# A chunked recurrence ahead of a mixture of experts: the start-up and the order within a unit are changed

## The chip, the cores and the metric

The kernel runs on one core of a Trainium2 chip. The metric is the device time of one execution in microseconds; the change is judged by the median of several runs beside runs of the kernel before. A profile of one execution shows the core's engines: PE (TensorE, matmuls), DVE (VectorE), ACT (ScalarE), POOL (GpSimd) and SP (SyncE, which here only issues transfers).

## What is computed

A linear recurrence with a decaying state per head, and then a mixture of eight experts with two chosen per token:

```python
def _attn_ref(r, k, v, w, a, b):            # 4 batches, 8 heads, 768 steps, 40 wide
    for t in range(S):
        y[:, :, t] = np.einsum('bhd,bhde->bhe', rt, state)
        Sa = np.einsum('bhde,bhe->bhd', state, at)
        state_decay = state * wt[:, :, None, :] - np.einsum('bhd,bhe->bhde', Sa, bt)
        state = state_decay + np.einsum('bhd,bhe->bhde', vt, kt)

def _moe_ref(x, w_gate, w_noise, noise, w1, w2):   # 3072 tokens, 320 wide, hidden 1024
    noisy_logits = x @ w_gate + np.log1p(np.exp(x @ w_noise)) * noise
    # the two largest of 8, softmax over the two, then for each expert e
    h = np.maximum(x[mask] @ w1[e], 0.0)
    out[mask] += top2_w[mask, k, None] * (h @ w2[e])
```

## The kernel before, in words

The 768 steps are cut into 12 chunks of 64, and the 32 sequences into two halves of 16. A chunk of one half is a unit; there are 24 units (NU), which go through one after the other, the halves in turn. Within a unit the recurrence is matrix work on 64 x 64 blocks.

For each unit u, ahead of time (up to LP = 8 units): w, a and kb (k and b) are loaded into rings; `ln` (ACT) takes the logarithm of w into one of two tiles L and uc; `sm` (PE) sums it along the chunk by a triangular matrix; `ex` (ACT) takes exp of the sum with either sign, and POOL copies one column of it to gam; `lc` (DVE, tile lm) takes the largest logarithm, for a check at the end. `aprod` and `kprod` (x = 1 and x = 0) multiply a and kb by these in place, on POOL in the loop and on DVE at the start. `LS` (PE) forms a triangular 64 x 64 matrix, its closure evicts it on ACT into la, `LSd` copies a quarter of it.

The inverses of these matrices are made for four units at a time: `xtr` (DVE transposes), `solve` (DVE, 30 elimination steps of two instructions, dealt out over the units by the tables PLAN and PLAN1 to three places A, B and C of a unit), `tout` (two DVE transposes back, and a POOL memset). `TA` and `TB` (PE) join 32-blocks to 64. The first four units take smaller blocks (`solve16`, 14 steps, `tout16`) and join them in `S16a` and `S16b` on PE with evictions on ACT between and after.

Unit n of the loop in `run` issues on PE, in this order: Y(n-1), W2(n), TA(n) with two fillers, LS(n+7), TB(n), AK(n+1), U(n), KBT(n+1), sm(n+8), UT(n), RL(n-1), W1(n+1), P(n), ST(n+1) with two fillers; up to n = 2 also S16(n+1) after P. A filler (`warm`) is a 128 x 512 matmul on zeros whose output nobody reads. Evictions follow on ACT: w of W2, two of TA (dr), tt of TB, ln(n+8), la of LS, uc and two pm of U, two utm of UT, kt of KBT, LSd, xr of RL, two exps of ex(n+8), z of S16a, two pm of vc, St of ST. On DVE stand the state's sum S and xT after Y, lc, akm after AK, the logit reduce lg after RL, pm after P, and the solve steps: C after Y, B before RL, A at the end of the unit. POOL scales the state by gam right after S, and does aprod and kprod and, from unit 9 on, the scatters of the routing.

The order on each engine is the order of the calls (`manual_schedule`); each engine and each queue works in that order, and `after` adds a wait on an instruction. `s.ea` is the last ACT instruction, on which loads of the loop are made to wait. PSUM has three tiles of the kind p2 and two of the kind p1.

Ahead of the loop `ramp` does constants, loads and the first four units, and ends in `first`, which is unit 0 with the products of units 4 to 8 in between. Behind unit 23 the experts follow; the tables for them are loaded in units 15 to 21.

## Time and profile before

| | us |
|---|---|
| median of 3 runs | 818.46 (816.27 to 822.21) |
| the profiled execution | 817.96 |
| its span, first to last instruction | 816.0 |
| start and units 0 to 3 (to the filler of unit 4's TA) | 116.5 |
| units 4 to 15 | 174.1 |
| units 16 to 23 and the joint with the experts (to 402) | 111.3 |
| the experts | 414.0 |
| busy over the span: PE, DVE, ACT, POOL | 728.5, 516.5, 391.0, 337.8 |

A matmul in float32 is recorded as several instructions, so sm's four are eight. In the views `rw` holds the ring of w, `ra` that of a, `rk` that of kb, and `X__71` the tile of the elimination. [...] The chain of waits goes back from the last instruction to what released each one.

### The profile page before, as it was taken

The numbers are of one execution on the slowest core, as the hardware profiler recorded it, in microseconds if no ns is written. First come the engines' busy times: TensorE is split into PE (matmuls) and PEld (weight loads), VectorE is DVE, ScalarE is ACT, GpSimd is POOL, SyncE is SP. The second block draws the span as 40 slices with busy tenths as digits, with TensorE's granted clock in tenths as the row PEclk, the third lists the DMA queues.
The fourth block names the chain that finished last, engine by engine and source line by source line (L and its number), as shares of the span: only waits on it lengthen the run. The fifth ranks groups of instructions, "written<-read, shape, count | busy, mean of one in ns | idle before, by whom it ended". The sixth has DMA issues, their size and how long they took to land.

```text
span 816.0 us, 29101 instructions
## 1 busy us (share of the span) xinstructions
PE 728.5 (89%) x12619; PEld 537.9 (66%) x12619; DVE 516.5 (63%) x1083; ACT 391.0 (48%) x837; POOL 337.8 (41%) x463
## 2 busy tenths in 40 slices
...
GB/s 203 57 163 112 106 135 140 159 137 156 119 143 143 168 125 58 107 125 82 92 74 100 163 71 184 111 122 114 134 94 144 20 124 117 41 13 26 28 18 40
DMA packets 67700, 87.06 MB, mean 107 GB/s; under 512 B 15641, under 2 KB 52461, under 8 KB 67565
## 3 DMA queue, kind: packets, MB, share of 16 engines
...
HBM read 63.41 MB, written 21.69 MB: 104 GB/s over the span
## 4 chain that ended last, share of the span: by engine, by line
PE 67%; DVE 14%; ACT 10%; issue 5%; DMA 2%; another core or an unknown queue 0%; SPq 0%; POOL 0%; ACTq 0%; DVEq 0%; POOLq 0%
PE po L369 21%; PE ph L354 21%; PE py L782 3%; PE sm L589 2%; PE pt L334 2%; DVE Tt L635 2%; DVE X__71 L636 2%; PE kt L710 2%; DVE pm L768 2%; PE tb L696 2%; PE pp L766 2%; ACT la L524 2%; PE ta L686 1%; PE rl L795 1%; DVE dr L639 1%
## 5 line engine op out<-in xcount | busy, mean ns | idle before, releaser
L377 POOL DMA_INDIRECT out_dram<-y,le x45 | 74.6, 1658 | 189.7 <-ACT y L371 186.6
L354 PE MATMUL ph<-rw__68,rk 128*128 128x384 f16 (+1 forms) x512 | 97.0, 339 | 3.7 <-DVE hl L356 1.8
L354 PE MATMUL ph<-dr,la 128*128 128x448 f16 (+1 forms) x384 | 85.8, 339 | 1.4 <-issue 1.4
L369 PEld LDWEIGHTS <-rk 128*128 128x128 f16 x576 | 56.5, 99 | 36.9 <-issue 7.3
L182 POOL DMA_INDIRECT ls<-ent,po x48 | 50.2, 1045 | 70.3 <-ACT pm L524 44.5
L354 PEld LDWEIGHTS <-rk 128*128 128x128 f16 x512 | 49.5, 98 | 40.5 <-issue 4.5
L371 ACT ACTIVATE y<-po,le 128x320 f32<-128x320 f32 (+1 forms) x53 | 26.6, 504 | 93.0 <-PE po L369 74.5
L356 DVE SCALAR_TENSOR_TENSOR hl<-ph,hh 128x448 f16<-128x448 f32 x64 | 39.2, 621 | 44.8 <-ACT hh L355 44.3
L355 ACT ACTIVATE hh<-ph 128x448 f16<-128x448 f32 x64 | 34.0, 543 | 64.8 <-PE ph L354 63.6
L636 DVE TENSOR_TENSOR X__71<-X__71,Tt 128x30 f32<-128x30 f32 (+9 forms) x150 | 60.8, 405 | 5.5
L635 DVE TENSOR_TENSOR Tt<-X__71 128x30 f32<-128x30 f32 (+9 forms) x150 | 60.8, 406 | 3.7
L355 ACT ACTIVATE rk<-ph 128x384 f16<-128x384 f32 x64 | 30.7, 488 | 62.5 <-PE ph L354 43.8
L242 DVE TENSOR_REDUCE yc<-y 128x1 f32<-128x320 f32 (+1 forms) x53 | 23.8, 456 | 57.3 <-ACT y L371 56.8
L369 PEld LDWEIGHTS <-hh 128*128 128x128 f16 (+1 forms) x640 | 46.5, 103 | 18.5 <-issue 2.0
L356 DVE SCALAR_TENSOR_TENSOR rk<-ph,rk 128x384 f16<-128x384 f32 x64 | 34.4, 552 | 34.0 <-ACT rk L355 22.5
L354 PEld LDWEIGHTS <-la 128*128 128x128 f16 x384 | 37.2, 98 | 27.3 <-issue 1.6
L782 PE MATMUL py<-pm,kt 128*64 128x104 f32 (+1 forms) x768 | 42.8, 262 | 7.3 <-DVE pm L768 3.8
L594 POOL COPY gam<-B 104x8 f32<-104x8 f32 x24 | 5.3, 220 | 105.7 <-ACT B L524 104.9
L369 PE MATMUL po<-ra,rk 128*128 128x320 f16 x288 | 46.0, 306 | 3.0 <-ACT rk L355 2.5
L782 PEld LDWEIGHTS py<-pm,kt 128*64 128x64 f32 x768 | 36.8, 142 | 10.9 <-DVE pm L768 5.0
L607 POOL TENSOR_TENSOR rk<-rk,B 104x512 f32<-104x512 f32 x31 | 36.9, 1189 | 13.2 <-DVE X__71 L636 9.0
L369 PE MATMUL po<-w2h,rk 128*128 128x320 f16 x192 | 33.7, 302 | 3.7 <-issue 2.6
...
## 6 DMA issues: line engine op xcount, KB each, us to landing
...
```

Source lines behind the costliest of these rows:

```text
L182: st=nc.gpsimd.indirect_dma_start(out=s.ls,out_offset=OFFS(ap=po[:,j,k:k+1],axis=0),in_=s.ent[:,j,k],in_offset=None)
L242: s.nc.vector.tensor_reduce(s.yc[q:128,s.ny:s.ny+1],a,axis=AX.X,op=ALU.add); s.ny+=1
L354: for i,(a,b) in enumerate(mm): s.hmm=nc.tensor.matmul(ph[:,:n],a,b,start=i==0,stop=i==7)
L355: s.hrelu=nc.scalar.activation(hh[:,f],ph[:,:n],AF.Relu)
L356: s.hhl=nc.vector.scalar_tensor_tensor(hl[:,f],ph[:,:n],0.0,hh[:,f],op0=ALU.max,op1=ALU.subtract)
L369: for j in range(c): nc.tensor.matmul(po[p*j:p*j+p,:d],h[:,f,r],w[:,f,d*j:d*j+d],start=k==0,stop=k==23)
L371: s.hy=nc.scalar.activation(y[:,:d],po[:,:d],AF.Copy,scale=w_[:,ii:ii+1])
L377: st=s.nc.gpsimd.indirect_dma_start(out=o[0],out_offset=OFFS(ap=o[1],axis=0),in_=o[2],in_offset=None,compute_op=ALU.add)
L607: s.after((eng or s.nc.gpsimd).tensor_tensor(z,z,b1,op=ALU.mult),e)
L635: eng.tensor_tensor(t,X[:,j:j+1,j+1:].to_broadcast([128,j,m]),X[:,0:j,j:j+1].to_broadcast([128,j,m]),op=ALU.mult)
L636: s.hs=eng.tensor_tensor(X[:,0:j,j+1:],X[:,0:j,j+1:],t,op=ALU.add)
L782: nc.tensor.matmul(pp[64*y:64*y+64,b,128*hh:128*hh+n],kt[:,j,y],m[:,y,j,0:n],start=first and hh==0,stop=True,skip_group_check=True)
```

## The change

**At the start.** Two w tiles are loaded first and each later w one unit earlier than before. Constants are cleared in another order, some by POOL rather than DVE or ACT; the clearing of vt, r and rb goes from ACT (`null`) to POOL. Five fillers on a cleared tile wz stand ahead of the first sm, two after most of the following steps (WU), and 24 (WR) between W1(0) and sm(6), while DVE eliminates. The loop over the first four units is written out as a pipeline: sm of the next unit goes ahead of the products of this one; the gamma copies of units 0 to 5 go to DVE.

**lc.** For units from 4 on the DVE reduce becomes a Square on ACT with the sum as a second output, ahead of the two exps in `ex`; units 0 to 3 keep the reduce (`lcv`).

**Joining.** S16 is taken apart: S16a stands behind KBT's eviction, S16b behind P.

**The unit.** ln, sm and ex of unit n+9 go to the end of unit n, behind ST; LSd follows LS's eviction at once. kprod x=1 of unit n+8 stands first in the unit and waits for the last A step of the unit before (hA), the scaling of the state (`Sg`) and aprod wait for the last C step, or for xT where there is none (hC), kprod x=0 waits for the logit reduce (hl). ST's fillers are kept only where no unit lies eight ahead, and unit 16 gets the four fillers FL too. In `first` P(0) comes ahead of the products of unit 7; unit 1 does sm, ex and kprod of unit 9 as well.

```diff
-FT,FS,FL,FU=2,2,4,2
+FT,FS,FL,FU,WR,W0,WU=2,2,4,2,24,5,2
-        s.z=t([128,160],F32,name="z"); V.memset(s.z,0.0)
-        s.d1=t([128,8,65],F16,name="d1"); s.mk32=t([128,1,32],F32,name="mk32")
+        s.d1=t([128,8,64],F16,name="d1"); s.wz=s.fl(s.d1)[:,0:128]; V.memset(s.wz,0.0); s.z=t([128,160],F32,name="z")
+        s.mk32=t([128,1,32],F32,name="mk32")
         s.L=[t([128,4,2,64],F32,name="L"),s.uc]; s.TR=t([128,136],F32,name="TR")
-        V.memset(s.a[0],0.0); V.memset(s.kb[0],0.0); V.memset(s.L[0],0.0); V.memset(s.a[1],0.0); V.memset(s.kb[1],0.0); V.memset(s.L[1],0.0)
+        V.memset(s.L[0],0.0); V.memset(s.a[0],0.0); V.memset(s.kb[0],0.0); V.memset(s.L[1],0.0)
         G.memset(s.TR,0.0)
-        G.memset(s.a[2],0.0); G.memset(s.kb[2],0.0); G.memset(s.gt,1.0); G.memset(s.lm,0.0); G.memset(s.a[3],0.0); G.memset(s.kb[3],0.0)
+        V.memset(s.z,0.0)
+        G.memset(s.a[1],0.0); G.memset(s.kb[1],0.0); G.memset(s.lm,0.0); G.memset(s.gt,1.0); G.memset(s.a[2],0.0); G.memset(s.kb[2],0.0); G.memset(s.a[3],0.0); G.memset(s.kb[3],0.0)
...
+        if i==2:
             for z in s.kt: G.memset(z,0.0)
-            G.memset(s.mk32,1.0)
-            for q in range(4): G.affine_select(out=s.mk32[32*q:32*q+32,0],in_=s.mk32[32*q:32*q+32,0],pattern=[[-1,32]],base=0,channel_multiplier=1,compare_op=ALU.is_gt,fill=0.0)
-            G.memset(s.d1,0.0)
-        if i==1:
-            for q in range(4): G.tensor_copy(s.i32[32*q:32*q+32],s.m.idm[32*q:32*q+32,32*q:32*q+32])
+            G.memset(s.fl(s.d1)[:,128:512],0.0)
             for z in s.w: G.memset(z,0.0)
-            G.memset(s.dg,0.0)
-        if i==2:
-            G.memset(s.rp,0.0); G.memset(s.iw,0.0)
+            G.memset(s.iw,0.0)
+    def warm0(s,pp,k):
+        for _ in range(k): s.nc.tensor.matmul(pp,s.wz,s.wz[:,0:1].to_broadcast([128,512]),start=True,stop=True)
...
     def lc(s,u):
-        s.nc.vector.tensor_reduce(s.lm[:,u:u+1],s.L[u%2 if u<7 else 0][...,0:40].rearrange("p h y e->p (h y) e"),axis=AX.XY,op=ALU.max,apply_absolute_value=True)
-    def sm(s,u):
-        pp=s.Sp=s.p1t("sm"); L=s.L[u%2 if u<7 else 0]
+        s.act(s.fl(s.wq[u%NW])[:,0:320].rearrange("p (h y e)->p h y e",h=4,y=2),s.L[u%2 if u<7 else 0][...,0:40],AF.Square,accum_out=s.lm[:,u:u+1])
+    def sm(s,u,t=None):
+        pp=s.Sp=s.p1t("sm") if t is None else t[:,0]; L=s.L[u%2 if u<7 else 0]
+    def lcv(s,u):
+        s.nc.vector.tensor_reduce(s.lm[:,u:u+1],s.L[u%2][...,0:40].rearrange("p h y e->p (h y) e"),axis=AX.XY,op=ALU.max,apply_absolute_value=True)
     def ex(s,u):
+        if u>3: s.lc(u)
         z=s.Sp.rearrange("p (j t)->p j t",t=64); B=s.B[u%2][:,0:520].rearrange("p (j c)->p j c",c=65)
         s.act(s.wq[u%NW][:,:,0:64],z,AF.Exp,scale=-1.0)
         s.act(B[:,:,0:64],z,AF.Exp)
-        s.nc.gpsimd.tensor_copy(s.gam[0:RF,u],B[0:RF,:,0])
+        if u>5: s.nc.gpsimd.tensor_copy(s.gam[0:RF,u],B[0:RF,:,0])
-    def aprod(s,u,eng=None,h=None):
-        R=slice(0,RF); h=slice(0,8) if h is None else slice(4*h,4*h+4); a=s.a[u%NAB][R,h]
-        (eng or s.nc.gpsimd).tensor_tensor(a,a,s.wq[u%NW][R,h,0:64],op=ALU.mult)
+    def aprod(s,u,eng=None,e=None):
+        R=slice(0,RF); a=s.a[u%NAB][R]
+        s.after((eng or s.nc.gpsimd).tensor_tensor(a,a,s.wq[u%NW][R,:,0:64],op=ALU.mult),e)
...
-        if u and u+LP<NU: s.sm(u+LP)
         pp=s.p1t("ut")
-        if not u or u+LP>=NU: s.warm(pp,FU)
+        if u+LP>=NU: s.warm(pp,FU)
...
-        pp=s.p1t("st"); s.warm(pp,FS); S=s.S[u%2]
+        pp=s.p1t("st"); s.warm(pp,FS if u+LP>=NU else 0); S=s.S[u%2]
...
-                nc.gpsimd.tensor_tensor(Sv,Sv,gb,op=ALU.mult)
-        nc.vector.tensor_tensor(x.rearrange("p (h b) t->p b h t",b=2),pv[...,0:64],s.wq[u%NW][:,:,0:64].rearrange("p (h b) t->p b h t",b=2),op=ALU.mult)
+                s.sg=(Sv,gb)
+        s.hx=nc.vector.tensor_tensor(x.rearrange("p (h b) t->p b h t",b=2),pv[...,0:64],s.wq[u%NW][:,:,0:64].rearrange("p (h b) t->p b h t",b=2),op=ALU.mult)
+    def Sg(s):
+        if s.sg is not None: s.after(s.nc.gpsimd.tensor_tensor(s.sg[0],s.sg[0],s.sg[1],op=ALU.mult),s.hC); s.sg=None
...
-            for u in us: load(u); s.lw(u+1)
+            for u in us: load(u); s.lw(u+2)
             s.ea=e
-        s.lw(0); loads(0,1,2,3); LS={}
-        s.ln(0); s.sm(0); s.ex(0); s.ln(1); s.sm(1); gn(4); s.consts1(0)
-        for u in range(4):
-            if u<3: s.ex(u+1)
-            s.aprod(u,V); s.kprod(u,1,None,V); s.kprod(u,0,None,V); s.lc(u)
-            if u==3: s.lc(4); V.tensor_reduce(s.m16,s.i32[:,16:32],axis=AX.X,op=ALU.add)
-            if u>1: s.lmask(u-2)
-            if u==0: loads(4); gn(5,6)
-            if u==1: s.consts1(1); gn(7,8)
-            if u==2: s.consts1(2); G.memset(s.a[9],0.0)
-            if u<3: s.ln(u+2); s.sm(u+2)
-            LS[u]=s.LS(u)
-            if u: LS[u-1](); s.LSd(u-1)
-        LS[3](); s.LSd(3); s.lmask(2); s.AK(0); s.lmask(3); s.ex(4); s.ln(5); s.sm(5); s.ex(5); s.xtr(0)
-        s.consts1(3); s.xmask16()
-        s.ea=None; s.lv(0); loads(5,6)
+        s.lw(0); s.lw(1); loads(0,1,2,3); LS={}
+        s.warm0(s.p1t("wm"),W0)
+        def vp(u): s.aprod(u,V); s.kprod(u,1,None,V); s.kprod(u,0,None,V); gc(u)
+        def gc(u): V.tensor_copy(s.gam[0:RF,u],s.B[u%2][0:RF,0:520].rearrange('p (j c)->p j c',c=65)[:,:,0])
+        f=s.p2("wm")[:,0]
+        s.ln(0); s.sm(0); s.Sq={0:s.Sp}; s.lcv(0); s.ln(1); s.warm0(f,WU); s.sm(1); s.Sq[1]=s.Sp; s.lcv(1); s.consts1(0)
+        def ex(u): s.Sp=s.Sq[u]; s.ex(u)
+        ex(0); vp(0); s.ln(2); s.warm0(f,WU); s.sm(2); s.Sq[2]=s.Sp; gn(4); ex(1); s.lcv(2); loads(4)
+        LS[0]=s.LS(0); vp(1); s.ln(3); s.sm(3); s.Sq[3]=s.Sp; LS[0](); s.LSd(0); s.consts1(1); G.memset(s.dg,0.0); s.warm0(f,WU)
+        ex(2); s.lcv(3); LS[1]=s.LS(1); vp(2); s.lmask(0); ex(3); LS[1](); s.LSd(1); gn(5); G.memset(s.rp,0.0); s.warm0(f,WU)
+        LS[2]=s.LS(2); V.tensor_reduce(s.m16,s.i32[:,16:32],axis=AX.X,op=ALU.add); vp(3); s.lmask(1); s.ln(4); LS[2](); s.LSd(2); s.warm0(f,WU); LS[3]=s.LS(3); s.AK(0); s.sm(4); s.lmask(2)
+        LS[3](); s.LSd(3); s.lmask(3); s.ex(4); s.ln(5); s.sm(5); gc(4); s.ex(5); s.xtr(0); gc(5)
+        s.consts1(2); gn(6); s.consts1(3); s.xmask16()
+        s.ea=None; s.lv(0); loads(5)
+        for z in s.vt+s.r[:1]+s.rb[:1]: G.memset(z,0.0)
+        gn(7,8)
+        for z in s.r[1:]+s.rb[1:]: G.memset(z,0.0)
+        G.memset(s.a[9],0.0)
         m.consts2(s.z)
-        s.KBT(0)(); s.consts16(); s.ln(6)
-        s.W1(0)
-        for z in s.vt+s.r+s.rb: s.null(z)
-        s.ea=None; H('gv',s.vt,0); H('gr',s.r,0); H('grb',s.rb,0); s.lv(1); load(7); s.lw(8); load(8)
+        s.KBT(0)(); s.consts16(); s.ln(6); s.W1(0)
+        s.warm(s.p1t("wm"),WR)
+        s.sm(6,s.p2("sm"))
+        s.ea=None; H('gv',s.vt,0); H('gr',s.r,0); H('grb',s.rb,0); s.lv(1); loads(6); load(7); load(8)
...
-        s.lw(LP+1); load(LP+1); H('gr',s.r,1); H('grb',s.rb,1); s.lv(2)
+        s.lw(LP+1); load(LP+1); H('gr',s.r,1); H('grb',s.rb,1); s.lv(2); s.lw(LP+2)
...
-        s.vprods(4); s.vprods(5); s.lc(5); s.lc(6)
-        s.S16a(0); s.S16b(0); s.sm(6); a4=s.LS(4); s.W2(0); s.ex(6); s.TA(0); a4(); s.ln(7); a5=s.LS(5); s.TB(0); s.vprods(6)
-        s.sm(7); a5(); s.U(0); s.LSd(4); k=s.KBT(1); s.UT(0); s.ex(7); s.lc(7); s.vprods(7)
-        a6=s.LS(6); s.LSd(5); k(); s.ln(LP); s.lc(LP)
-        s.P(0); s.S16a(1); a6(); s.LSd(6); s.AK(1); s.Y(0); a7=s.LS(7); s.S16b(1); s.sm(LP); a7(); s.LSd(7); s.ex(LP)
+        s.vprods(4); s.vprods(5)
+        s.S16a(0); s.S16b(0); a4=s.LS(4); s.W2(0); s.ex(6); s.TA(0); a4(); s.ln(7); a5=s.LS(5); s.TB(0); s.vprods(6)
+        s.sm(7); a5(); s.U(0); s.LSd(4); k=s.KBT(1); s.UT(0); s.ex(7)
+        a6=s.LS(6); s.LSd(5); k(); s.ln(LP)
+        s.P(0); s.vprods(7); s.S16a(1); a6(); s.LSd(6); s.AK(1); s.Y(0); a7=s.LS(7); s.S16b(1); s.sm(LP); a7(); s.LSd(7); s.ex(LP)
         s.ld(H,1,'gv',s.vt)
-        s.xtr(1); s.xmask(); s.aprod(LP,V); s.kprod(LP,1,None,V)
-        s.W1(1); s.vc(1); s.hA=None
+        s.xtr(1); s.xmask(); s.aprod(LP,V); s.kprod(LP,1,None,V); s.kprod(LP,0,None,V)
+        s.ln(LP+1); s.W1(1); s.vc(1); s.lnx=LP+1; s.hA=None
...
-            if n and ok(n+LP-1): s.kprod(n+LP-1,0,s.hA)
+            if ok(n+LP) and n>1: s.kprod(n+LP,1,s.hA)
+            s.hs=s.hx
             if n>1: s.Y(n-1); sv('C')
+            s.hC=s.hs
+            if n>1: s.Sg()
             if n and not q and n<=20: m.rstep()
             if ok(n): s.W2(n); s.TA(n)
-            s.ld(s.lw,n+LP+1)
+            if n==1: s.sm(LP+1); s.ex(LP+1); s.kprod(LP+1,1)
+            s.ld(s.lw,n+LP+2)
             ls=s.LS(n+LP-1) if n>1 and ok(n+LP-1) else None
-            if n>1 and not ls: s.warm(s.p2('wm')[:,0],FL)
+            if not ok(n+LP): s.warm(s.p2('wm')[:,0],FL)
...
             if ok(n): s.TB(n)
-            if n and ok(n+LP): s.ln(n+LP); s.lc(n+LP)
-            if ls: ls()
-            if ls and not q: s.LSd(n+LP-1)
+            if ls: ls(); s.LSd(n+LP-1)
+            if n==1: s.LS(LP)(); s.LSd(LP)
...
-            if n and ok(n+1): s.AK(n+1)
+            if ok(n+1): s.AK(n+1)
+            if ok(n+LP): s.aprod(n+LP,None,s.hC)
...
-            if n==1: ls=s.LS(LP); ls()
             if kb: kb()
-            if ls and q: s.LSd(n+LP-1)
+            if n<3: s.S16a(n+1)
...
-            if n==NU-1: s.turn(0); s.act(s.gt[:,8*NU:9*NU],s.lm,AF.Exp)
+            if n==NU-1: s.turn(0); s.act(s.gt[:,8*NU:8*NU+4],s.lm[:,0:4],AF.Exp); s.act(s.gt[:,8*NU+4:9*NU],s.lm[:,4:NU],AF.Exp,scale=0.03)
...
             if ok(n-1): s.RL(n-1)
             cut()
             sc(1)
-            if n and ok(n+LP): s.ex(n+LP); s.kprod(n+LP,1)
             if ok(n+1): s.W1(n+1)
+            if ok(n+LP): s.kprod(n+LP,0,s.hl)
             if ok(n): s.P(n)
-            if ok(n+LP): s.aprod(n+LP)
-            if n<3: s.S16(n+1)
+            if n<3: s.ln(n+1+LP); s.S16b(n+1)
...
             sv('A'); s.hA=s.hs
             if solving and q==3: s.tout()
             s.ld(s.lv,n+2)
+            if ok(n+1+LP) and n>=3: s.ln(n+1+LP)
             if ok(n+1): s.ST(n+1)
+            if ok(n+1+LP): s.sm(n+1+LP); s.ex(n+1+LP)
```

## Rows read from the trace of the kernel before

**Rows 1.** Windows: busy time (instructions) of PE, PEld, DVE, ACT, POOL, clock, DMA.
```profile
66.94:85.08 18.14, 16.17 (x521) 13.61 (x517) 15.09 (x31) 11.06 (x27) 7.08 (x8) 0.88 0.34 104
...
103.21:116.53 13.32, 12.70 (x394) 10.99 (x388) 10.71 (x25) 8.66 (x20) 3.51 (x5) 1.00 0.38 111
116.53:290.67 174.14, 155.97 (x4676) 134.63 (x4671) 146.63 (x334) 105.51 (x248) 83.24 (x117) 0.99 0.51 147
...
402.00:816.00 414.00, 384.94 (x2813) 247.72 (x2804) 219.12 (x402) 156.07 (x295) 162.65 (x144) 0.98 0.40 87
```

**Rows 2.** Windows over two stretches at a low granted clock, the columns as before.
```profile
34.00:47.00 13.00, 6.54 (x202) 5.62 (x202) 12.08 (x23) 9.61 (x21) 4.14 (x26) 0.50 0.38 121
...
64.00:68.00 4.00, 4.00 (x55) 2.77 (x52) 1.67 (x1) 3.76 (x10) 0.19 (x1) 0.57 0.23 62
```

**Rows 3.** Timeline of the start: begin, us, engine, line, operation, out<-in, count, idle before.
```profile
0.80 1.28 ACT L528 ACT_TABLE_LOAD   x1 [0.80 <-PEq L1083]
...
3.90 2.04 PE L589 MATMUL sm<-TR,L 128*128 128x128 f32 x8 [3.90 <-POOL lm L539]
...
22.40 0.60 ACT L524 ACTIVATE la<-ls 128x512 f32<-128x512 f32 x1 [1.90 <-PE ls L614]
23.02 0.84 ACT L524 ACTIVATE la<-la 32x256 f32<-32x256 f32 x2
...
28.26 0.15 DVE L657 TENSOR_TENSOR Tt<-X__71 128x28 f32<-128x28 f32 x1
...
38.14 1.14 ACT L544 ACTIVATE r<-z 128x512 f32<-128x512 f32 x2
...
40.26 1.11 DVE L664 MEMSET dr<- 32x512 f32 x2 [0.16 <-DMA vt<-in_gv_dram]
...
47.36 0.69 PE L686 MATMUL ta<-dr,la 32*32 32x32 f32 x32
...
55.22 0.69 DVE L601 TENSOR_TENSOR ra<-ra,rw__68 104x512 f32<-104x512 f32 x1 [4.66 <-ACT rw__68 L524]
55.83 1.29 DVE L607 TENSOR_TENSOR rk<-rk,B 104x512 f32<-104x512 f32 x2
...
58.19 1.22 DVE L768 TENSOR_TENSOR pm<-pp,mk 128x1024 f32<-128x1024 f32 x1
```

**Rows 4.** Chain of waits at the start: begin, us, what.
```profile
3.44 4.07 DMA rw__68<-in_gw_dram
```

**Rows 5.** Chain of waits in unit 1, around S16.
```profile
77.53 0.49 ACT B L524
...
80.38 0.54 PE st L568 x2
```

**Rows 6.** Chain of waits in unit 6.
```profile
149.73 0.89 PE sm L589 x8
...
153.72 0.54 PE st L568 x2
...
155.32 1.58 PE py L782 x32
```

**Rows 7.** Chain of waits in unit 10.
```profile
201.22 0.61 DVE xT L792
...
203.34 0.48 ACT L L524
...
203.84 0.48 DVE lm L586
...
205.01 0.59 DVE akm L707
```

**Rows 8.** Timeline of unit 6, then a group by form (count, sum, mean ns).
```profile
154.77 1.18 POOL L607 TENSOR_TENSOR rk<-rk,B 104x512 f32<-104x512 f32 x1
...
154.94 1.25 DVE L635 TENSOR_TENSOR Tt<-X__71 128x220 f32<-128x220 f32 x1
...
L635 DVE TENSOR_TENSOR Tt<-X__71 128x240 f32<-128x240 f32 x10 | 4.0, 404 | 0.2
```

6 lines of the change are left out of this document (5 added, 1 removed).

## The prediction, made before the result was known

> **What bounds the kernel now.** I read the windows first. Attention fills the span to about 402 us; the experts take the other 414 us and no line of theirs is edited [rows 1]. So the change can only move the left part, and the experts' start moves with it. Inside attention there are two unlike stretches. Up to 116.5 us, four units are solved at start-up and units 0 to 3 go through; units 1 and 2 last 18.1 us each, unit 3 13.3 us. Units 4 to 15 take 174.1 us, 14.5 us each, with PE busy 156 and DVE 147 of them [rows 1].
>
> At the start no engine is full. PE is slow: eight sm matmuls take 2.04 us there and 0.89 us in unit 6 [rows 3, 6]. [...] The chain from 0 to 41 us then alternates between ACT, PE's sm and, from 28.3 to 41.4, DVE's elimination with its transposes [rows 3].
>
> In units 4 to 8 the chain runs along PE, one unit after another, with hardly a gap; a filler of 0.54 us before ST stands in it [rows 6]. In units 9 to 15 it runs along DVE. Unit 10 shows why: after xT, DVE waits through TB, its eviction and ACT's ln for the lm reduce, and akm starts 3.2 us after xT ended [rows 7].
>
> **A. To the start of the elimination (28.26 us now).** w of units 0 and 1 are issued together, so ln(1) no longer waits for a load that was issued at 3.44 and landed 4.07 us later [rows 4]; now ln(2) is the first that waits for such a load, to about 7.6. POOL clears a1 and kb1 now and each load still stands behind its own memset, so SP's order costs nothing that the w2 load doesn't show. From there ACT's list is what is left: ln of units 2 to 5 (4 x 0.48), pairs of exp for units 1 to 5 (5 x about 1.0), the evictions of LS with their copies (4 x (0.60+0.84)), two Squares and the last sm's wait (about 1.5) [rows 3, 5, 7]. That is 14.2 us, to 21.8; the gamma copy and the mask on DVE add 0.6. The elimination would start near 22.4, not 28.26: 5.8 us. This needs the fast PE. If the fillers don't raise the clock, six sm (12.4) and fifteen fillers of about 0.5 (1.0 for a pair at the low level, twice the 0.54 of [rows 6]) stand on PE from 3.9 on, and the gain is 0 to 2. I take **4.0**, nearer to the list, as loads may be late.
>
> **B. Elimination to TA(0) (28.26 to 47.36).** DVE's part, to 41.37, is untouched [rows 3]. After it PE now does S16b, sm(6), LS(4) and fillers, all at the low clock, for 6.0 us. The 24 new fillers and sm(6) run under DVE's 13.1 us and cost nothing there; without that cover they would cost 24 x 0.27 = 6.5 us. The five clearings (0.57 each, of which [rows 3] has two) go from ACT to POOL: they held back S16a's eviction, and SP's loads of v, r and rb stand behind POOL's memsets now. POOL is through with them by about 30 by my addition, earlier than the 38 to 40 on ACT. What is left after DVE: the products of unit 4 (0.69+0.64, first of the two kprods [rows 3]), LS(4) of about 0.7, the filler pair 0.54: 2.0 to 2.6 us rather than 6.0. I take **3.0**; 2.5 if the clock is low then.
>
> **C. TA(0) to unit 3.** In `first`, pm(0) stands on DVE behind the products of unit 7, which wait for their exp till 55.22, and starts at 58.19 [rows 3]; P comes before them in the new order: up to 2.7 us. The joining: in unit 1 the chain has 2.4 us between the end of the exp and ST, S16's two halves with an eviction between them [rows 5]; unit 2 shows 2.3. With S16a before RL and S16b after P, RL, W1 and P lie over that eviction. [...] Against this unit 1 gets sm and ex of unit 9 as well (0.9 on PE, some 1.5 on ACT). With the stalls gone the units should come near unit 3's present 13.3 [rows 1]: 18.14+18.13-13.5-13.3 = 9.5, and 2 in `first`: 11.5. Bounds: 5, if the low stretches stay, and 15. I take **9.5**.
>
> **D. Units 3 to 15, and the later ones.** Removed from PE: a filler pair of 0.54 per unit up to 14. sm moves behind ST, into the time in which PE waits for pm in any case: pm takes 1.2 [rows 3], and fillers, ST and Y's first half now fill 1.6 between P and Y's second half [rows 6]. But sm needs ln(n+9), which is behind vc on ACT. ACT works 8.8 us a unit (105.5 over 12 [rows 1]); by my estimate three quarters of it stand in one unbroken list from tt to that ln, and L is ready some 0.5 us after ST has ended, so PE waits there: of the 0.54 I count 0.3 in units 4 to 8, 1.5 us. Removed from DVE: the lm reduce of 0.48 and its wait. In unit 10 akm could start when AK is through, some 1.5 us sooner [rows 7]; where PE binds instead, nothing. Added to ACT: a Square with a sum. No row shows one; the bounds are 0.48 (the ln of the same size [rows 7]) and twice that, if the sum is a piece of its own, and I take 0.5, hidden, as ACT is busy 106 of 174 us [rows 1].
>
> POOL's products now wait for DVE: kprod x=1 for the last step of the elimination, the state's scaling and aprod for the C steps, kprod x=0 for the logit reduce. Behind them on POOL stand the scatters; LS a unit later and ST wait for the products, with over 3 us to spare. On SP the w load of unit n+10 takes the ring's place of unit n-1 and so waits for xT at the start of unit n; the loads of a, kb, r and v behind it are needed a unit or more later, so I count nothing. What POOL's waits may give: a DVE step of 220 elements took 1.25 us beside a POOL kprod of 1.18, where one of 240 takes 0.40 on average [rows 8]; each such meeting costs DVE some 0.85, and three products a unit can meet it. Beside S, xT and pm, which read PSUM, it is not seen (pm 1.22 [rows 3]). [...]
>
> Units 9 to 15: 1.0 us each, 7. Minus 1.0 for a set of four fillers new in unit 16, minus 0.5 for odds and ends: **7.0**. Bounds: -3 (fewer fillers, two more falls of the clock at 1.7 us, nothing else gained) and +15. Units 17 to 23 keep all their fillers and I count nothing.
>
> **The sum.** 4.0+3.0+9.5+7.0 = 23.5 us off the span of 816.0 gives 792.5. The median shown, 818.46, is 2.5 above that span (the profiled execution itself is given as 817.96): **795.0**. The parts' bounds are unlikely to fall together; the likeliest case's own range is 783 to 804.
>
> **Rivals.** *The unit's new order gives nothing.* sm at the end waits for ACT, fewer fillers let the clock fall more often. [...] Against: DVE's chain in units 9 to 15. Then D is -3: 805.
>
> *The start stays slow.* The fillers don't bring the clock up, or let it fall before DVE is through. For: from 34 to 47 us PE worked half the time and stayed at the low level. Against: from 64 to 68 it was busy throughout and the clock came back inside that stretch [rows 2]. Then A is 0, B 2.5, C 6: 803. With both, 813.
>
> *Slower: the Square needs another table.* The trace has one table load, 1.28 us at the start [rows 3], for Ln, Exp and Copy. If Square is not in that set, two loads stand before each pair of exp from unit 4 on, 2.6 us on ACT in some 20 units. ACT's 8.8 us a unit plus 0.5 plus 2.6 still fits 13, but ex comes right before W2's eviction: 0.8 to 2.6 us a unit, 16 to 51 in all, so 811 to 846, say 830. It decides once two loads exceed the 2 us or so that ACT has free there. [...]
>
> **How the numbers follow.** The likeliest case 0.57, the order gives nothing 0.16, the start stays slow 0.11, both 0.09, the table 0.05, something else 0.02. A measurement here can tell about 1%, so faster is below 810.3 and slower above 826.6. The first three cases are faster; so is a third of "both"; the rest of it and a little of the table case are within 1%. Faster 0.87, same 0.08, slower 0.05. The range goes from the likeliest case's low end over both single rivals: 783 to 809.
>
> **What would show it.** A: the elimination's first step near 24 us, sm near 0.9 to 1.1 us from the second or third on. B: TA(0) near 40. [...] D: units 4 to 8 near 13.0, units 9 to 15 about 1 us shorter each, DVE's steps of 220 elements near 0.4. Wrong if table loads appear, if a unit's chain shows PE waiting for L before sm for over 1 us, or if PE's clock falls inside units 4 to 15 more than twice.

## The result, and the profile after

| | before | after |
|---|---|---|
| median, us | 819.63 (4 runs) | 806.83 (805.41 to 810.29, 4 runs) |
| ratio after/before, 95% interval | | 0.986 (0.981 to 0.991) |
| span of the profiled execution | 816.0 | 804.0 |
| elimination's first step | 28.26 | 30.45 |
| TA(0): its first filler | 46.40 | 46.01 |
| TA(3): the same | 103.21 | 102.19 |
| units 4 to 15 | 174.14 | 163.42 |
| units 16 to 22 | 103.00 | 102.48 |

The forecast was 795.0 with a range of 783 to 809. The sign was right. The time lies in the range, but above the 804 of the likeliest case and only because the range reached over the rivals: the span fell by 12.0 us, not 23.5. Nearly all of it, 10.7 us, came from units 4 to 15. The start and units 0 to 2, for which A, B and C had promised 16.5, gave 1.0.

Windows of the kernel after; the columns are those of [rows 1]: length, busy time (instructions) of PE, PEld, DVE, ACT, POOL, granted clock (of PE, as a share of its full speed), DMA share, GB/s.

```profile
65.52:84.26 18.74, 16.23 (x528) 14.17 (x523) 14.41 (x31) 15.21 (x39) 6.11 (x9) 0.91 0.33 99
84.26:102.19 17.93, 16.07 (x552) 13.87 (x547) 11.10 (x26) 10.31 (x26) 4.60 (x5) 0.90 0.39 114
102.19:115.27 13.08, 12.64 (x392) 10.84 (x386) 10.80 (x24) 9.23 (x22) 4.10 (x5) 1.00 0.44 138
115.27:278.69 163.42, 153.99 (x4646) 131.62 (x4641) 130.37 (x322) 109.80 (x267) 82.44 (x116) 1.00 0.52 153
390.00:804.00 414.00, 384.90 (x2799) 247.46 (x2797) 218.75 (x401) 156.25 (x295) 162.68 (x144) 0.98 0.39 87
```

Units 1 and 2 (first two rows) are as long as before, with PE busy for 16 us in each. In units 4 to 15 DVE lost 16 us of work and PE fills 94% of the time. The experts' 414 us are the same work as before.

Timeline of the start of the kernel after (begin, us, engine, line, operation, out<-in, count, idle before):

```profile
5.57 1.05 PE L591 MATMUL sm<-TR,uc 128*128 128x128 f32 x8
...
14.23 1.29 DVE L612 TENSOR_TENSOR rk<-rk,B 104x512 f32<-104x512 f32 x2
14.23 0.52 POOL L818 MEMSET ra<- 128x512 f32 x1
14.70 0.95 POOL L818 MEMSET rk<- 128x1024 f32 x1
...
17.37 1.86 POOL L556 MEMSET kt<- 128x1024 f32 x2
...
17.76 0.58 DVE L826 COPY gam<-B 104x8 f32<-104x8 f32 x1
...
21.30 0.94 POOL L818 MEMSET rk<- 128x1024 f32 x1
21.52 8.44 DVE L826 COPY gam<-B 104x8 f32<-104x8 f32 x1 [1.28 <-ACT B L524]
21.60 8.36 DVE L630 STREAM_TRANSPOSE X__71<-la 128x1024 f32<-128x1024 f32 x1
22.19 0.98 POOL L565 MEMSET S<- 128x512 f32 x2
...
29.12 0.52 POOL L840 MEMSET ra<- 128x512 f32 x1
...
30.45 0.15 DVE L662 TENSOR_TENSOR Tt<-X__71 128x28 f32<-128x28 f32 x1
```

The pipeline itself worked: the second sm already took 1.05 us, and at 21.5 everything for the transpose was ready. Then DVE's COPY of eight columns stood for 8.44 us, the transpose with it, while POOL cleared tile after tile; both ended at 29.96, when POOL's long clearings were through. The two products of two inputs at 14.23 took 1.29 us beside such clearings, as did the pair at 55.83 in the kernel before [rows 3], with POOL idle but for a copy that ended at 55.96. An earlier gamma copy, at 17.76, ended at 18.34, right behind the first of kt's two clearings (17.37 to 18.32), although the second followed without a gap: that COPY got in between the two.

Units 0 to 2 have pauses of PE of another kind, which the view puts down to "issue", a wait for nothing that the profile shows:

```profile
61.57 0.21 PE L683 MATMUL sb<-w1s 32*32 32x16 f32 x3
63.59 0.17 PE L683 MATMUL sb<-w1s 32*32 32x16 f32 x1 [1.81 <-issue]
...
68.25 1.16 PE L591 MATMUL sm<-TR,L 128*128 128x128 f32 x8 [1.50 <-ACT L L524]
...
96.69 0.33 PE L760 MATMUL st<-idm,S 128*128 128x128 f32 x1 [1.44 <-issue]
96.81 2.04 PE L591 MATMUL sm<-TR,L 128*128 128x128 f32 x8
```

The first stands in the middle of S16b(1), the other right behind S16b(3). After the one, ACT's late list makes sm(9) wait 1.50, and the granted clock is 0.57 on average from 69 to 73 us; after the other it is 0.50 from 97 to 99, and sm takes 2.04 again. I call the pauses without a releaser "stops".

### The profile page after: what moved, and what is told of

It reads as the page before. It is cut to its first block, busy times and chain, and to the rows that moved or that the text cites. A ratio compares the mean times of both kernels' runs of the same rounds, so it can differ in the third digit from the quotient of the medians.

```text
span 804.0 us, 29172 instructions
## 1 busy us (share of the span) xinstructions
PE 728.4 (91%) x12632; PEld 531.1 (66%) x12632; DVE 501.4 (62%) x1069; ACT 399.6 (50%) x873; POOL 339.3 (42%) x463
## 4 chain that ended last, share of the span: by engine, by line
PE 71%; DVE 12%; ACT 8%; issue 5%; POOL 2%; DMA 0%; another core or an unknown queue 0%; ACTq 0%; DVEq 0%; POOLq 0%
PE po L369 22%; PE ph L354 20%; PE py L786 3%; PE pp L770 3%; PE pt L334 2%; PE rl L801 2%; PE tb L701 2%; PE ta L691 2%; ACT la L524 2%; ACT dr L524 2%; PE sm L591 1%; DVE Tt L640 1%; PE ut L749 1%; PE pw L723 1%; PE pw L732 1%
## 5 line engine op out<-in xcount | busy, mean ns | idle before, releaser
L369 PEld LDWEIGHTS <-rk 128*128 128x128 f16 x576 | 56.7, 100 | 36.6 <-issue 6.6
L640 DVE TENSOR_TENSOR Tt<-X__71 128x30 f32<-128x30 f32 (+9 forms) x150 | 55.7, 372 | 3.7
L641 DVE TENSOR_TENSOR X__71<-X__71,Tt 128x30 f32<-128x30 f32 (+9 forms) x150 | 49.8, 332 | 5.5
L786 PE MATMUL py<-pm,kt 128*64 128x104 f32 (+1 forms) x768 | 40.5, 254 | 4.1 <-issue 2.7
L772 DVE TENSOR_TENSOR pm<-pp,mk 128x1024 f32<-128x1024 f32 x24 | 29.4, 1223 | 16.5 <-PE pp L770 15.8
L786 PEld LDWEIGHTS py<-pm,kt 128*64 128x64 f32 x768 | 34.7, 137 | 7.4 <-issue 4.3
```

The lines of the kernel that those rows point to most:

```text
L369: for j in range(c): nc.tensor.matmul(po[p*j:p*j+p,:d],h[:,f,r],w[:,f,d*j:d*j+d],start=k==0,stop=k==23)
L640: eng.tensor_tensor(t,X[:,j:j+1,j+1:].to_broadcast([128,j,m]),X[:,0:j,j:j+1].to_broadcast([128,j,m]),op=ALU.mult)
L641: s.hs=eng.tensor_tensor(X[:,0:j,j+1:],X[:,0:j,j+1:],t,op=ALU.add)
L772: nc.vector.tensor_tensor(m.rearrange("p y j x->p (y j) x")[...,0:64],pp.rearrange("p y (j t)->p (y j) t",t=64),s.mk.to_broadcast([128,16, ...
L786: nc.tensor.matmul(pp[64*y:64*y+64,b,128*hh:128*hh+n],kt[:,j,y],m[:,y,j,0:n],start=first and hh==0,stop=True,skip_group_check=True)
```

## The experiments

The runs were timed in five groups, each beside the kernel before. On the chips of the first four that kernel takes 799 to 800 us, on that of the last 822, so times are compared as ratios to it. The intervals are 0.3 to 0.7% to each side, so most single steps are read from the traces (one execution each). In the table "elimination from" is the start of its first step, and TA(0) and TA(3) stand for the start of their first filler, in us:

| run | ratio, 95% | elimination from | TA(0) | TA(3) | units 4 to 15 |
|---|---|---|---|---|---|
| g1, the changed kernel | 0.986 (0.982 to 0.991) | 31.28 | 46.84 | 103.98 | 163.8 |
| a1 | 0.982 (0.975 to 0.989) | 24.75 | 40.37 | 98.14 | 163.1 |
| a2 | 0.978 (0.972 to 0.983) | 25.50 | 41.42 | 98.05 | 163.7 |
| c1 | 0.987 (0.983 to 0.992) | 30.85 | 46.91 | 110.07 | 163.6 |
| d1 | 0.984 (0.978 to 0.989) | 31.05 | 46.62 | 102.00 | 164.7 |
| d2 | 0.988 (0.982 to 0.993) | 30.91 | 46.49 | 102.69 | 170.0 |
| d3 | 0.983 (0.978 to 0.987) | 31.00 | 46.81 | 104.76 | 164.2 |
| e1 | 0.979 (0.974 to 0.983) | 26.12 | 41.75 | 97.33 | 167.0 |
| e4 | 0.983 (0.978 to 0.988) | 25.01 | 41.12 | 101.91 | 166.5 |
| f1 | 0.977 (0.972 to 0.982) | 25.41 | 41.22 | 94.91 | 163.7 |
| f2 | 0.973 (0.968 to 0.978) | 25.41 | 41.12 | 95.17 | 162.1 |
| f4 | 0.971 (0.966 to 0.976) | 27.32 | 42.91 | 98.89 | 162.8 |
| g2 | 0.977 (0.973 to 0.981) | 24.31 | 40.76 | 98.48 | 164.0 |
| h1 | 0.978 (0.975 to 0.981) | 25.17 | 40.95 | 94.08 | 163.8 |
| h2 = f2 again | 0.978 (0.975 to 0.981) | 25.88 | 41.11 | 97.32 | 163.6 |

How far one execution goes: f2 and h2 are the same program and take 54.1 and 56.2 us from TA(0) to TA(3); the changed kernel takes 56.2 and, as g1, 57.1. In this stretch a difference of some 2 us between two traces is not yet the effect of an edit.

**Who holds the COPY.** a1 makes it a product, a2 keeps it and holds POOL:

```diff
-V.tensor_copy(s.gam[0:RF,u],z[:,:,0])
+V.tensor_tensor(s.gam[0:RF,u],z[:,:,0],z[:,:,64],op=ALU.mult)
```

```diff
-for z in s.kt: G.memset(z,0.0)
+for z in s.kt: s.after(G.memset(z,0.0),s.hg)
```

(in a1 for units 4 and 5; in a2 `hg` is the gamma copy of unit 5)

> The changed kernel with one edit: the gamma copies of units 4 and 5 on DVE are a product of two SBUF inputs (B's column by B's column of ones) instead of a COPY; the result is the same. In the changed kernel the COPY of unit 4 stood from 21.52 to 29.96 us while POOL ran about 18 clearings without a gap, and the transpose behind it ended with it; the elimination began at 30.45. Theory (only the COPY is held by POOL's clearings; products of two inputs and the transpose are not): the product takes about 0.2 us, the transpose 2.0 from about 21.7, and the elimination begins at 25.5 to 26.0, as soon as the pair of exps of unit 5 is through (25.2). All that follows comes 4.5 us earlier, time about 802, against the kernel before 0.980. Rival (whatever stands on DVE there is held by POOL's clearings, the transpose too): the elimination still begins at 29.5 to 30.5, time about 807, 0.986.

> The changed kernel with one edit: the COPY stays, but POOL's clearings from those of kt on wait until the gamma copy of unit 5 on DVE is done; POOL has nothing to do from about 17.4 us to then. Theory (the clearings without a gap hold the COPY): the COPY takes 0.2 us, the elimination begins at 25.5 to 26.0 us. POOL's clearings and the loads of vt, r and rb behind them come 8 us later, so that part of the gain may be lost again behind the elimination: time 802 to 807. Rival (POOL has nothing to do with the 8.44 us, DVE waits for something the trace doesn't show, say ACT or a load): the COPY still ends near 30, and the time is 807 or more.

Timeline of a1, DVE:

```profile
21.48 0.17 DVE L829 TENSOR_TENSOR gam<-B 104x8 f32<-104x8 f32 x1 [1.28 <-ACT B L524]
21.57 1.99 DVE L630 STREAM_TRANSPOSE X__71<-la 128x1024 f32<-128x1024 f32 x1
...
24.75 0.15 DVE L662 TENSOR_TENSOR Tt<-X__71 128x28 f32<-128x28 f32 x1
```

And of a2:

```profile
22.18 0.17 DVE L826 COPY gam<-B 104x8 f32<-104x8 f32 x1 [1.28 <-ACT B L524]
22.26 1.95 DVE L630 STREAM_TRANSPOSE X__71<-la 128x1024 f32<-128x1024 f32 x1
```

Both cures work: the gamma product took 0.17 us beside the clearings (a1), the COPY 0.17 with POOL held (a2), so the 8.44 needed the COPY and POOL's unbroken clearings together. The transpose is not held (1.99 us in a1 beside the same clearings, 1.95 in a2 without them), so it only stood behind the COPY. By what mechanism the clearings hold the COPY no view shows; it waited through all of POOL's clearings from 21.5 to 29.9, not through one. In six traces with the COPY left in place it stood for 6.2 to 9.2 us there, while the earlier gamma copies took 0.2 to 1.2, once 2.8 (d2), and those beside POOL ended right behind an instruction of its; why the later row of clearings let none in stays open. TA(0) comes 6 us earlier in a1. From there to TA(3) it takes 57.8 us, the changed kernel 56.2 and, as g1, 57.1: up to 1.6 us of the gain are given back, with five stops of 6.1 us in sum. In time a1's interval is too wide to tell it from g1.

**What the stops are.** c1 puts 32 more fillers before sm(6). e1 (on a1) moves S16b away from the dense stretches (the second diff; in `first` behind sm(LP)), e4 (on a1) joins S16 again in units 1 and 2 (the third):

```diff
-FT,FS,FL,FU,WR,W0,WU=2,2,4,2,24,5,2
+FT,FS,FL,FU,WR,W0,WU=2,2,4,2,56,5,2
```

```diff
-if n<3: s.ln(n+1+LP); s.S16b(n+1)
+if n<3: s.ln(n+1+LP)
...
 if ok(n+1+LP): s.sm(n+1+LP); s.ex(n+1+LP)
+if n<3: s.S16b(n+1)
```

```diff
-if n<3: s.S16a(n+1)
...
-if n<3: s.ln(n+1+LP); s.S16b(n+1)
+if n<3: s.ln(n+1+LP); s.S16(n+1)
```

> [...] In the changed kernel PE did nothing from 34 to 40.4 and the granted clock was 0.50 from 35.7 to 48.9. Theory (that low stretch is paid for behind the elimination): the granted clock stays 1.00 up to unit 0, S16a takes 0.73 instead of 1.08, LS(4) 0.69 instead of 1.23, and TB(0) starts 1.5 to 2 us earlier; if nothing else takes it back, 805. Rival (unit 0 and 1 hang on ACT and on the stall of 1.8 us in S16b at 61.8, not on PE's speed): the clock is high, but TA(1) is not more than 0.5 us earlier, time 806 to 807. The 32 more fillers also move every later PE instruction against whatever sets the two stalls of 1.8 and 1.4 us without a releaser; if these depend on the count of PE instructions, they move to other places or change in size.

> The changed kernel with the gamma product of the run a1 and one more edit: S16b stands behind sm of the unit ahead (192 PE instructions in 1.0 us behind 16 that take 1.1), in unit 0 and in units 1 and 2, and no longer right behind LS or P (64 and 128 instructions of 64x64 in 0.7 and 1.5 us). In all runs so far every stop of PE without a releaser ended 2.4 to 2.9 us (a few 3.1 to 3.6) after a 16 KB packet of the instruction queue, and lay in or behind a stretch of 250 or more PE instructions in about 2.5 us. Theory (PE runs ahead of its code there): the stops shrink; a1 had 6.1 us of them in units 0 to 2 (0.96, 1.29, 1.67, 0.71, 1.44), here at most 3.5, and TA(3) comes 2 to 4 us earlier than a1's 98.1. Rival (the stops follow the number of instructions passed, whatever stands there, or S16b's evictions are late for TA): the stops stay at 5 to 7 us in sum, or TA waits for dr: TA(3) at 97.5 or later.

> The changed kernel with the gamma product of the run a1 and one more edit: in units 1 and 2 the joining is whole again, S16a right ahead of S16b, both behind P, with ACT's eviction of 0.28 us between them (unit 0 as in a1). Theory of the forecast (the two parts save the eviction's time on the path): units 1 and 2 become 0.5 to 1.2 us longer each, TA(3) 1 to 2.4 us later than in a1 (98.1). Rival (in parts or whole, PE runs out of code there, and the wait for the eviction only takes the place of such a stop): units 1 and 2 the same within 0.5 us in sum, with stops without a releaser of other sizes.

In c1 the clock was still 1.00 at 40 us, but S16a had to wait 3.67 us for DVE and took 1.05 all the same (mean clock 0.68 from 40 to 42 us, 0.50 behind that), and there were five stops at new places. TA(3) came 6 us later than in g1, which neither theory had expected. The last two of them, from the timeline of PE:

```profile
83.55 0.21 PE L682 MATMUL sb<-w1s 32*32 32x16 f32 x4 [1.39 <-issue]
...
102.28 0.18 PE L682 MATMUL sb<-w1s 32*32 32x16 f32 x1 [2.55 <-issue]
```

In e1 the stops of 0.55 us or more from TA(0) to TA(3) are two, 1.28 us in sum, against 6.1 in a1, with the same instructions; from TA(0) to TA(3) it takes 55.6 us, a1 57.8. That fits the theory and doesn't settle it: the same sum is 1.9 to 6.1 in the nine traces of the new order with S16b in its place and 0.6 to 3.8 in the six with S16b late.

In e4 one stop is left (0.97), but S16b waits 0.39 us for the eviction in each of units 1 and 2, and the way from TA(0) to TA(3) takes 60.8, 3.0 more than in a1. Most of that is the clock of this execution: in unit 2, which is 2.8 us longer than a1's, it is 0.82 against 1.00, and PE is busy 17.5 us with the work that takes 14.8 there. So in two parts is better, as the forecast said, by the 0.4 us a unit of that wait; more isn't shown.

The DMA view of the changed kernel from 56 to 68 us shows what the stops go with (its second row has 40 slices of 0.3 us; q8 is the instruction queue):

```profile
GB/s 0 0 55 0 0 0 0 0 0 0 0 0 0 0 0 55 0 0 0 0 0 0 0 0 0 0 0 0 55 0 0 0 0 0 0 0 0 0 0 0
q8 instruction: 3, 0.05, 1.9%
```

Three packets of 16 KB start at 56.7, 60.7 and 64.6, and PE goes on at 63.59, 2.9 us after the second. The 17 traces have 44 stops of 0.55 us or more from TA(0) to TA(3): 36 ended 2.2 to 2.9 us after the start of the last packet before them, as 15% of all moments would, five 3.0 to 3.6 and three elsewhere. Between the stops at 61.8 and 95.2 the view counts 2032 matmuls and weight loads of PE and eight packets, 254 instructions to a packet; S16b alone is 192 in 1.0 us. So stops and packets go together in time. That PE runs out of code there, as the theory has it, is not shown: it stands in no row, and no run changed the supply of code itself.

**ACT at the end of unit 0.** In e1 ACT stood idle for 4.51 us, to 60.36, with S16b's eviction first in its list, and sm(9) waited 2.34 us for ln(9) and then took 2.08; f1 puts other work ahead:

```diff
-a7=s.LS(7); s.sm(LP); s.S16b(1); a7(); s.LSd(7); s.ex(LP)
+a7=s.LS(7); s.sm(LP); a7(); s.LSd(7); s.lc(LP); s.S16b(1); s.ln(LP+1); s.ex(LP,False)
```

> e1 and one more edit, in unit 0 on ACT alone: the eviction of LS(7) with its copy and the Square of unit 8 come ahead of S16b's three evictions, and ln of unit 9 ahead of the exps of unit 8. [...] Theory (after the stops of PE, ACT's list at the end of unit 0 is what holds units 0 and 1): sm(9) starts 2 to 2.6 us earlier, the elimination's transpose at 59.6 to 60 instead of 62.59, units 0 to 2 together 2.5 to 4 us shorter than e1's 55.6. Rival (PE's own work and the stops set units 0 to 2): less than 1 us, the wait turns up before TA(1) or TB(1).

Timeline of e1, then of f1, then windows of f1 over units 1 and 2:

```profile
60.36 0.70 ACT L524 ACTIVATE dr<-sb 128x128 f32<-128x128 f32 x3 [4.51 <-PE sb L683]
...
64.67 2.08 PE L591 MATMUL sm<-TR,L 128*128 128x128 f32 x8 [2.34 <-ACT L L524]
```

```profile
60.03 1.95 DVE L630 STREAM_TRANSPOSE X__71<-la 128x1024 f32<-128x1024 f32 x1 [1.05 <-ACT la L524]
...
63.08 1.16 PE L591 MATMUL sm<-TR,L 128*128 128x128 f32 x8 [0.39 <-ACT B L524]
```

```profile
61.47:79.25 17.78, 15.16 (x523) 12.97 (x522) 14.22 (x31) 13.98 (x35) 6.79 (x9) 1.00 0.36 106
79.25:94.91 15.66, 14.81 (x552) 12.71 (x547) 10.84 (x26) 10.21 (x26) 3.85 (x5) 1.00 0.42 127
```

The transpose comes 2.6 us earlier, sm(9) 1.6 (TA(0) had come 0.5 earlier), and units 0 to 2 take 53.7 us, 1.9 less: between the two expectations, nearer to the theory's, though no more than two executions of f2 differ by. The two windows show units 1 and 2 at a granted clock of 1.00: PE's own work is 15.2 and 14.8 us.

**Fillers.** f2 (on f1) fills PE up to S16a (30 before sm(6), 8 behind), g2 (on f2) adds 8 before LS(4). f4 (on a1) and h1 (on f2) leave out W0 and WU; h2 is f2 beside h1.

```diff
-FT,FS,FL,FU,WR,W0,WU=2,2,4,2,24,5,2
+FT,FS,FL,FU,WR,W0,WU=2,2,4,2,30,5,2
...
-s.sm(6,s.p2("sm"))
+s.sm(6,s.p2("sm")); s.warm(s.p1t("wm"),8)
```

```diff
-s.S16a(0); s.S16b(0); a4=s.LS(4)
+s.S16a(0); s.S16b(0); s.warm(s.p1t("wm"),8); a4=s.LS(4)
```

```diff
-FT,FS,FL,FU,WR,W0,WU=2,2,4,2,30,5,2
+FT,FS,FL,FU,WR,W0,WU=2,2,4,2,30,0,0
```

(f2, g2, h1; f4 as h1 with 24)

> f1 and one more edit: 30 fillers instead of 24 before sm(6) and 8 behind it, so that PE has no pause over 1 us from 24 us on to S16a at 35 to 36. In a1 and e1 PE stood for 1.1 to 1.9 us before sm(6) and 2.1 before S16a, and the granted clock was 0.50 from about 33 to 46. Theory (the low stretch costs S16a 0.32, S16b 0.4, LS(4) 0.5, the filler pair 0.5, TA 0.35, LS(5) 0.4, TB 0.5): from S16a's start to TB(0)'s end 1.5 to 2.5 us less than in f1. Rival (ACT and DVE set this stretch, as c1 suggests, where 32 more fillers gained nothing before TA(1)): 0 to 0.7 us. The 76 more instructions move the stops without a releaser, by up to 2 us either way.

> f2 (gamma product, S16b behind sm, ACT's order in unit 0, fillers up to S16a) and 8 more fillers between S16b(0) and LS(4), where PE waited 2.0 us for DVE in f2. Theory (the clock's fall behind S16a costs unit 0): the granted clock stays 1.00 up to TB(0), LS(4) takes 0.69 instead of 1.23, TB 0.7 instead of 1.16, TA(1) comes 1.5 to 2.5 us earlier than in f2 (61.4), and the time is 0.968 to 0.973 against the kernel before. Rival (ACT's and DVE's lists set unit 0): the clock is high, TA(1) at most 0.5 us earlier, 0.972 to 0.976. Either way 1.0 to 1.5% faster than the changed kernel.

> a1 without the fillers ahead of the first sm and between the steps of the first four units (W0 and WU 0; WR stays). Theory of the forecast (they bring the clock up; without them sm takes 2.04 us six times and the start gains 0 to 2 us): sm of units 1 to 3 takes 1.8 to 2.1 us, the elimination begins at 27 to 29 us instead of 24.75, time 2 to 4 us longer than a1. Rival (the start hangs on the loads of w at 3 us a unit and on ACT's list, sm lies beside them): sm takes 2 us but the elimination begins before 26, time within 1.5 us of a1.

> f2 without the fillers ahead of the first sm and between the steps of the first four units. Theory of the forecast (the early fillers bring the clock up, and the start gains by it): the elimination begins 2 to 3 us later than in f2 (25.4), and with it TA(3), time 2 to 3 us longer than f2's. Rival (later starts are given back in units 0 and 1, where ACT's list and PE's supply of code set the pace): the elimination begins 2 to 3 us later, TA(3) at most 1 us later, the time within 1.5 us of f2's.

> f2, unedited, beside h1: elimination from 25.4, TA(3) at 94.5 to 96, 0.970 to 0.976 against the kernel before.

f2 doesn't shorten the way from S16a's start to TB(0)'s end (9.5 us against 9.6) nor that from TA(0) to TA(3) (54.1 against 53.7). g2 keeps the clock at 1.00 from 28 to 52 us and LS(4) takes 0.69, but PE then stops in P, S16a and AK, and TA(1) comes at 62.87, later than f2's 61.43 (h2, the same program as f2, has 63.90):

```profile
51.27 1.36 PE L676 MATMUL sa<-dr,w1s 32*32 32x16 f32 x52 [0.65 <-issue]
...
55.19 0.37 PE L710 MATMUL ak<-ra,rk 64*64 64x64 f32 x1 [1.03 <-issue]
```

In this execution the faster PE only came sooner to where it stops. g2's ratio, 0.977, and h2's, 0.978 with TA(3) at 97.32, lie above all that was expected of them (0.976 and 96 at most).

Without the early fillers sm became short all the same: it took 1.16 at the third and fourth in f4 and at the fifth in h1. In f4 the fifth and sixth took 2.07 and 2.08 again, and the elimination began 2.6 us later than in a1; f4 was not slower in its median. h1 began it no later than f2 and h2 and has h2's ratio. The early fillers are worth nothing that can be measured in the time.

**Units 4 to 15.** Three edits of the changed kernel, each undone alone: d1 the lm reduce on DVE again (from unit 9), d2 no waits of POOL, d3 ST's fillers kept. g1 is the control.

```diff
-if u>3: s.lc(u)
+if 3<u<=LP: s.lc(u)
...
-if ok(n+1+LP) and n>=3: s.ln(n+1+LP)
+if ok(n+1+LP) and n>=3: s.ln(n+1+LP); s.lcv2(n+1+LP)
```

```diff
-if ok(n+LP) and n>1: s.kprod(n+LP,1,s.hA)
+if ok(n+LP) and n>1: s.kprod(n+LP,1)
...
-if ok(n+LP): s.aprod(n+LP,None,s.hC)
+if ok(n+LP): s.aprod(n+LP)
...
-if ok(n+LP): s.kprod(n+LP,0,s.hl)
+if ok(n+LP): s.kprod(n+LP,0)
```

```diff
-pp=s.p1t("st"); s.warm(pp,FS if u+LP>=NU else 0); S=s.S[u%2]
+pp=s.p1t("st"); s.warm(pp,FS); S=s.S[u%2]
```

(`lcv2` is the reduce on unit u's L; in d2 the scaling `Sg` doesn't wait either)

> The changed kernel itself, unedited, on the chip of the experiments. Every theory: 0.983 to 0.988 against the kernel before, elimination from 29.5 to 31.5 us, TA(0) near 46 to 47, TA(3) at 102 to 103, units 4 to 15 in 163 to 165 us.

> The changed kernel with one edit: from unit 9 on the sum for the range check is again the lm reduce on DVE (0.48 us a unit, directly behind ln, at the end of the unit) instead of the Square on ACT. Theory (as in the forecast: in units 9 to 15 DVE's list sets the pace and this edit carried much of the gain): units 9 to 15 are 0.5 to 1.0 us longer each, units 16 to 22 at most 0.5, 4 to 8 us in all: 811 to 815, against the kernel before 0.990 to 0.995. Rival (the gain of units 4 to 15 came from POOL's products waiting for DVE, and from sm's new place): at most 0.2 us a unit, 807 to 809.

> The changed kernel with one edit: POOL's three products and the scaling of the state no longer wait for DVE's last step, xT or logit reduce; they run as soon as their data are there, in the new order. In the changed kernel the elimination steps of units 4 to 15 took 105 us in 266 instructions, 7 us over the shortest of their sizes; before it were 20 us over. Theory (the waits took POOL's reads of SBUF out of DVE's elimination steps, and that gave most of the 10.7 us of units 4 to 15): the excess of the steps goes back to 15 to 20 us and units 4 to 15 become 6 to 10 us longer, 813 to 817 on the chip where the changed kernel had 806.8, against the kernel before 0.993 to 0.998. Rival (the gain came from sm, ln and exps in their new place, by which PE no longer waits, and the steps had slack): units 4 to 15 at most 2 us longer, 0.986 to 0.989.

> The changed kernel with one edit: ST's pair of fillers is kept in all units (0.54 us on PE, ahead of ST). Theory (in units 3 to 15 PE's list sets the pace at 13.05 to 13.4 us, so the pair counts in full where DVE isn't later): units 3 to 15 are 0.3 to 0.54 us longer each, 4 to 7 us, 0.991 to 0.995 against the kernel before. Rival (the pair lies in the time in which PE waits for pm or L anyway, or keeps the clock up): at most 1.5 us, 0.986 to 0.988.

Units 4 to 15 took 163.8 us in g1, 164.7 in d1, 170.0 in d2, 164.2 in d3. Thirteen traces have the changed kernel's code in these units: they lie between 162.1 and 167.0, units 4 to 12 alone between 120.5 and 122.5, units 13 to 15 between 41.5 and 45.4. d1 and d3 lie inside that spread, but for d3's units 4 to 12, just above it with 122.6; d2 lies outside. Groups of the elimination's first instruction over units 4 to 15, changed kernel, then d2 (busy us, mean ns | idle):

```profile
L640 DVE TENSOR_TENSOR Tt<-X__71 128x30 f32<-128x30 f32 (+14 forms) x90 | 35.1, 391 | 2.2
```

```profile
L640 DVE TENSOR_TENSOR Tt<-X__71 128x30 f32<-128x30 f32 (+14 forms) x90 | 40.2, 447 | 2.2
```

With the second instruction of each step the 180 took 78.5 us before, 65.0 after and 82.6 in d2 (the 105 us of the expectation were counted over all units). The 6 us of d2 are lost in units 13 to 15 alone (48.8 against 42.9 in g1; 3.4 to 7.3 by the spread). Units 4 to 12 lose 0.3, although their steps take 12.7 us more (55.6 against 43.0): the chain runs mostly along PE there. In time d2 is not told apart from g1 (0.988 and 0.986).

From the kernel before to the changed one, units 13 to 15 gave 4.3 of the 10.7 us and units 4 to 12 gave 6.4. The waits bear on the 4.3; the 6.4 no single undoing brings back. d1 brings back the reduce, but not the wait ahead of it. The reduce over units 4 to 15 before, then in d1:

```profile
L586 DVE TENSOR_REDUCE lm<-L 128x1 f32<-128x320 f32 x12 | 5.8, 486 | 10.3 <-ACT L L524 10.2
```

```profile
L593 DVE TENSOR_REDUCE lm<-L 128x1 f32<-128x320 f32 x12 | 5.7, 474 | 0.0
```

Before, DVE stood idle for 10.3 us between xT and akm until ACT's ln was there, and akm came 4.2 to 7.1 us after TA's first filler; in the changed kernel it comes after 3.3 to 5.6. So the 6.4 us may come from the end of this wait or from the new place of sm, ln and exps; neither was undone alone.

## Why the prediction was right or wrong

**A, 4.0 forecast, -2.2 measured: wrong.** The step that failed is "the gamma copy and the mask on DVE add 0.6": the COPY took 8.44 us. It was moved from POOL, where it can't meet POOL's clearings, to DVE, where it did. The forecast had both halves, the copy here and, in B, POOL clearing until about 30, but reckoned with POOL's products alone in DVE's way, by the 1.25 us of [rows 8]. Without the COPY the elimination starts at 24.75 (a1), near the forecast's 24. Of the premise "this needs the fast PE" one trace without the early fillers says no (h1, 25.17) and one yes (f4, 27.32).

**B, 3.0 forecast, 2.6 measured: right.** From the first step to TA(0)'s first matmul behind the fillers 16.5 us instead of 19.1, with the clock at 0.50 from 35.7 us on, for which 2.5 was named; a1 shows the same (16.6).

**C, 9.5 forecast, 0.6 measured: wrong.** "The units should come near unit 3's present 13.3" left out PE's own work: S16's 320 instructions and, in unit 1, a second sm (named with 0.9, though the sum gives that unit only 0.2 more) and LS. At a granted clock of 1.00 it is 15.2 and 14.8 us (f1), so 26.8 for both was out of reach; the best run has 33.4. The rest went into the stops (1.8 and 1.4), ACT's list behind the first, and the clock that fell after both (0.57 from 69 to 73 us, 0.60 from 97 to 101); sm(9)'s 1.50 us for L is one of the signs that the forecast had named against itself. What the stops wait for is not shown. That S16 in two parts saves a wait was right, but it is 0.39 us a unit that shows (e4).

**D, 7.0 forecast, 11.5 measured with units 3 and 16 to 22: direction right, sizes in part.** Units 9 to 15 gave 7.4 where 7 stood in the sum, units 4 to 8 gave 3.3 where 1.5 stood; they came to 13.06 to 13.39, as forecast. The 1.0 us each of units 9 to 15 was mainly for the reduce off DVE and its wait: the reduce itself is worth at most 0.9 for all of them (d1), and the wait no run brought back, so by what mechanism the 7.4 came is open. POOL's waits, which I let stand at "what may give", hold some 6 in units 13 to 15 (d2).

**Rivals.** "The order gives nothing" and the table load fell: there is one load, 1.28 us at 0.81, and no second, and the Square took 0.47 and 0.19 for its sum, between the bounds. "The order gives nothing" is nearest in its sum (805), by luck: D gave more than forecast, not less, and A and C fell short. The 1.7 us for a fall of the clock, which this rival's -3 counts, no run shows; what the changed kernel shows is a granted clock of 1.00 over units 4 to 15. "The start stays slow" (803) names the right stretch, but not the mechanism: the second sm, at 5.57, already took 1.05 us, and DVE was held (8.44).

**A version that beats both.** h1 (gamma product, S16b late, ACT's order, fillers up to S16a, no early fillers) takes 802.9 us beside 822.0, 0.978 (0.975 to 0.981), where the changed kernel had 0.986 (0.981 to 0.991). The step is 0.8% and the two intervals meet at 0.981; f2 and f4 lie as low.
